# Decode attention on one core: one staging copy on POOL in place of four, and the last result copied and sent by ACT

## The chip, the cores and the metric

The kernel runs on one core of one Trainium2 chip. The metric is the device time of one execution in microseconds (us). Before the change it was 246.51 us, the median of three runs (246.47 to 246.59). Differences in this study are tenths of a microsecond, about 0.1%, so kernels are compared within rounds on the same chip, five executions each.

Engines are called PE (matmul; PEld is its weight load), DVE (vector), ACT (scalar), POOL (GpSimd) and SP (which issues 29 of this kernel's 31 DMAs). The *span* runs from the first to the last instruction of the kernel in the profile and is given to 0.1 us. The time is longer than the span (246.43 us against 244.6 us in the profiled run of the kernel before). The difference is called "outside the span" below.

## The reference

Two decode attentions, A and B, stand side by side, each with one query token of width 576, 32 query heads, 16 key/value heads of width 128 and a cache of 8192 keys. A looks at the last 2048 keys only, B at all of them.

```python
# x: [1,1,576]; k_cache, v_cache: [1,16,8192,128]; wq: [576,4096]; wo: [4096,576]
q = (x @ wq).reshape(1, 1, 32, 128).transpose(0, 2, 1, 3)
k = jnp.repeat(k_cache[:, :, Sk - W:, :], 2, axis=1)      # A: W = 2048; B: all 8192
v = jnp.repeat(v_cache[:, :, Sk - W:, :], 2, axis=1)
p = softmax(jnp.einsum("bhqd,bhkd->bhqk", q, k) * 128 ** -0.5)
o = jnp.einsum("bhqk,bhkd->bhqd", p, v)
out = o.transpose(0, 2, 1, 3).reshape(1, 1, 4096) @ wo     # A and B are joined
```

## The kernel before

The work runs in five groups: group 0 is all of A, groups 1 to 4 are four key/value heads of B each. The keys of a group lie in two slots. PE turns key blocks, ACT and DVE copy the turned blocks out of PSUM, PE multiplies them with the queries (the scores), softmax follows, and PE multiplies with the values. At the end the output weights are applied, for A (`P = 0`) and then for B (`P = 1`).

Before the scores of a slot can run, POOL puts the queries of that slot into a sparse matrix `qst`, in four small copies:

```python
def q_stage(g, s):
    def go(pool):
        for e in range(2):
            for x in range(2):
                o = s * 514 + e * 260 + x * 128
                if g:      # a group of B
                    dst = bass.AP(tensor=qst, offset=o, ap=[[1024, 128], [40, 4], [1, 2]])
                    src = bass.AP(tensor=qcol, offset=HQ + 8 * (g - 1) + 4 * e + 2 * s,
                                  ap=[[2 * HQ, 128], [0, 4], [1, 2]])
                else:      # A
                    ...    # cut: the same with another pattern
                ins = pool.tensor_copy(dst, src)
        return ins
    add("pool", go, reads=[("qcol", min(g, 1))], writes=[("qst", s)], tag="q%d" % s)
```

`add` records the instruction with what it reads and writes, and the semaphores follow from that. The results leave like this:

```python
def finish_out(P):
    n = OUTS[P]
    add("dve", lambda dve: dve.tensor_copy(outsb[0:32 * n, P, 0:DM // n], ktps[P][0:32 * n, 0:DM // n]),
        reads=[("bank", P)], writes=[("outsb", P)])
    def put(eng):
        ...                # cut: source and destination of 1152 bytes
        return eng.dma_start(dst, src)
    add("sp", put, reads=[("outsb", P)], writes=[("out", P)], dma="out%d" % P)

# cut: after all is recorded
prog.emit()                # every engine's program; at its end a barrier of all engines
for P in range(2):
    o = prog.writer[("out", P)]
    nc.sync.wait_ge(prog.sem(o.key), o.value)       # SP waits for both outputs to land
```

Of the kernel before, what the change touches and what calls it, by code (L numbers as in the profile page):

```python
# [7 lines left out]
ACT = mybir.ActivationFunctionType  # L8
AX = mybir.AxisListType

HQ = 32
HKV = 16
DH = 128
DM = 576
# [22 lines left out]
class Program:  # L37
# [15 lines left out]
    def add(self, eng, fn, reads=(), writes=(), dma=None, after=(), tag=None, inc=1, loop=None):  # L53
        op = Op(eng, fn, tuple(reads), tuple(writes), dma, tag, inc if dma is None or inc > 1 else 16, loop)
        deps = []
        for r in op.reads:
            w = self.writer.get(r)
            if w is not None:
                deps.append((w, True))
            if r[0] == "bank":  # L60
                deps += [(o, False) for o in self.readers.get(r, ())]
        for r in after:
            deps += [(o, False) for o in self.readers.get(r, ())]
        for r in op.writes:
            w = self.writer.get(r)
            if w is not None:
                deps.append((w, False))
            deps += [(o, False) for o in self.readers.get(r, ())]
        for r in op.reads:
            self.readers.setdefault(r, []).append(op)  # L70
        for r in op.writes:
            self.writer[r] = op
            self.readers[r] = []
        for o, raw in deps:
            if o is op:
                continue
            if o.dma is None and o.eng == eng and (not raw or eng in ("pe", "sp")):
                continue
            op.deps.append(o)
            o.needed = True  # L80
        op.order = len(self.ops)
        self.ops.append(op)
        return op
# [192 lines left out]
def bass_concat_heads__sliding_block_cached__gqa_block_cached__decode_kernel(  # L276
# [30 lines left out]
    prog = Program(nc)  # L307
    add = prog.add
# [14 lines left out]
    qst = nc.alloc_sbuf_tensor("qst", [128, 1024], BF16)  # L323
    qcol = nc.alloc_sbuf_tensor("qcol", [128, 2, HQ], BF16)
# [15 lines left out]
    outsb = nc.alloc_sbuf_tensor("outsb", [128, 2, DM // 2], BF16)  # L340
    warm = nc.alloc_sbuf_tensor("warm", [128, 8], F32)

    ktps = [nc.alloc_psum_tensor("ktps%d" % b, [128, 512], F32) for b in range(4)]
# [73 lines left out]
    def load_v(g):  # L417
# [19 lines left out]
        reads=["ident"], writes=["twice"])  # L437
    add("pe", lambda pe: pe.matmul(misc[:, 320:338], lhsT=twice[:, :], rhs=xnine[:, :, :].rearrange("p a r -> p (a r)"),  # L438
                                   start=True, stop=True),
        reads=[("xnine", 0), ("xnine", 1), "twice"], writes=[B_M])  # L440
# [34 lines left out]

    def q_stage(g, s):
        def go(pool):
            for e in range(2):
                for x in range(2):
                    o = s * 514 + e * 260 + x * 128  # L480
                    if g:
                        dst = bass.AP(tensor=qst, offset=o, ap=[[1024, 128], [40, 4], [1, 2]])
                        src = bass.AP(tensor=qcol, offset=HQ + 8 * (g - 1) + 4 * e + 2 * s, ap=[[2 * HQ, 128], [0, 4], [1, 2]])
                    else:
                        dst = bass.AP(tensor=qst, offset=o, ap=[[1024, 128], [80, 2], [40, 2], [1, 2]])
                        src = bass.AP(tensor=qcol, offset=8 * x + 4 * e + 2 * s, ap=[[2 * HQ, 128], [16, 2], [0, 2], [1, 2]])
                    ins = pool.tensor_copy(dst, src)  # L487
            return ins
        add("pool", go, reads=[("qcol", min(g, 1))], writes=[("qst", s)], tag="q%d" % s)
# [206 lines left out]

    def finish_out(P):
        n = OUTS[P]
        add("dve", lambda dve: dve.tensor_copy(outsb[0:32 * n, P, 0:DM // n], ktps[P][0:32 * n, 0:DM // n]),  # L699
            reads=[("bank", P)], writes=[("outsb", P)])  # L700

        def put(eng):
            src = bass.AP(tensor=outsb, offset=P * DM // 2, ap=[[32 * DM, n], [1, DM // n]])
            dst = out[0, 0:1, P * DM:(P + 1) * DM].rearrange("o (j n) -> (o j) n", j=n)
            return eng.dma_start(dst, src)
        add("sp", put, reads=[("outsb", P)], writes=[("out", P)], dma="out%d" % P)


    WQ = [(4 * SLOT - WQ_W, [("v", 2)]), (SLOT, [("k", 1, 0), ("k", 1, 1), ("v", 0)])]
    for P in range(2):  # L710
# [11 lines left out]
        reads=["kindA"], writes=["sameA"])  # L722
# [3 lines left out]
        reads=["sameB0"], writes=["sameB"])  # L726
# [3 lines left out]
    def pick_A(dve):  # L730
# [8 lines left out]
        reads=["sameB0", "pickB"], writes=["pickB"])  # L739
# [3 lines left out]
        reads=["four"], writes=["maskP"])  # L743
# [35 lines left out]
    for P in range(2):  # L779
        for Q, lo, n, off, res in wo_loads:  # L780
            if Q == P:
                wo_part(P, lo, n, off, res)
        finish_out(P)
    prog.emit()
    for P in range(2):
        o = prog.writer[("out", P)]
        nc.sync.wait_ge(prog.sem(o.key), o.value)

# [1 line left out]
_INS = ['A_x', 'A_k_cache', 'A_v_cache', 'A_wq', 'A_wo', 'B_x', 'B_k_cache', 'B_v_cache', 'B_wq', 'B_wo']  # L790
# [24 lines left out]
```

## Time and profile before

| | before |
|---|---|
| time, median of 3 runs | 246.51 us |
| span of the profiled run | 244.6 us (its time: 246.43 us) |
| read from memory | 102.76 MB, 420 GB/s over the span |
| PE, DVE, ACT, POOL busy | 67%, 36%, 38%, 4% |
| staging copies on POOL | 40, of 191 ns |

First, lines of the page: the busy time of each engine, then, in 40 equal slices of the span, the busy share of the DMA engines in tenths, then the queue that carries the loads with its packets, megabytes and share of time.

```profile
PE 163.9 (67%) x2325; PEld 119.5 (49%) x2325; DVE 88.2 (36%) x152; ACT 92.5 (38%) x95; POOL 9.1 (4%) x57
DMA  8999999999999999899999999998989999989993
q1 hardware_dynamic: 3900, 102.76, 98.1%
q14 instruction: 2, 0.02, 0.0%
```

The digits of 8 and 9 say that the loads hardly pause (their queue holds 98.1% of the DMA engines' time), and no engine comes near 100% (PE has 67%): the kernel is bound by its loads. Only in the last slice do they run out (a digit of 3). The line of queue 14 counts two fetches of instructions.

Next, the table of windows: for each stretch the busy time of each engine with its number of instructions, the granted PE clock, the DMA share and the rate in GB/s.

```profile
core 0: us, PE busy (x) PEld busy (x) DVE busy (x) ACT busy (x) POOL busy (x), PEclk, DMA share, GB/s
178.00:217.00 39.00, 29.87 (x397) 21.61 (x394) 15.01 (x22) 17.59 (x18) 0.00 (x0) 0.80 1.00 432
233.00:242.50 9.50, 6.95 (x204) 5.49 (x200) 2.35 (x4) 0.00 (x0) 0.00 (x0) 1.00 0.78 322
242.50:244.60 2.10, 0.02 (x4) 0.00 (x0) 0.31 (x1) 0.00 (x0) 0.00 (x0) 1.00 0.00 1
```
After 242.5 us no load moves any more, only the last result is left. Then POOL's timeline, four copies merged into a line (start, length, instruction, and in brackets the idle time before and who ended it), and the list of waits for the same copies (total us, times, longest):

```profile
48.92 0.56 POOL L487 COPY qst<-qcol 128x8 bf16<-128x8 bf16 x4 [23.68 <-PE sacc L522]
62.63 0.56 POOL L487 COPY qst<-qcol 128x8 bf16<-128x8 bf16 x4 [13.15 <-PE sacc L522]
```

```profile
POOL qst L487 <- PE sacc L522: 145.2, 8, 30.9
```

POOL waits for PE's scores, since the queries of the group before are in use until then. Nobody is listed as waiting for POOL. Last, the end of the timeline: PE's last products, the copy out of PSUM, and the issue of the last DMA.

```profile
241.33 1.19 PE L691 MATMUL ktps<-slots,opj 128*32 128x144 bf16 x46 [0.72 <-issue]
242.57 0.31 DVE L699 CAST outsb<-ktps 128x144 bf16<-128x144 f32 x1 [2.78 <-PE ktps L691]
242.91 0.57 SPq L705 DMA_DIRECT2D out_dram<-outsb  x1
```

### The profile page before, as it was taken

How to read it: one execution, taken by the hardware profiler on the slowest of the kernel's cores; microseconds unless marked ns; L12 is line 12 of the kernel's file. 1: busy time of each engine (PE TensorE's matmuls, PEld its weight loads, DVE VectorE, ACT ScalarE, POOL GpSimd, SP SyncE). 2: the span in 40 equal slices, each digit the busy share in tenths (PEclk: the TensorE clock that was granted, in tenths of full speed). 3: DMA queues.
4: the chain of work that ended last, by engine and by line, in shares of the span. 5: the costliest groups of instructions: out<-in, count | busy, mean ns of one | idle time of the engine just before them, and what ended most of it. 6: DMA issues, size and time to landing. Idle time of an engine off the chain costs nothing. (4 is left out here: it accounts for less than half of the span.)

```text
span 244.6 us, 5235 instructions
## 1 busy us (share of the span) xinstructions
PE 163.9 (67%) x2325; PEld 119.5 (49%) x2325; DVE 88.2 (36%) x152; ACT 92.5 (38%) x95; POOL 9.1 (4%) x57
## 2 busy tenths in 40 slices
PE   0007339968389995393999162999457799945965
PEld 0002139746236773233866121987232787624854
DVE  0001306854316454204655302455322245543031
ACT  2000016855306786102876300687600378630000
POOL 5000100000000000000000000000000000000000
PEclk9999957997759999569999859799957589975599
DMA  8999999999999999899999999998989999989993
GB/s 313 458 404 419 431 434 426 429 426 431 450 426 430 482 397 461 375 434 429 489 429 429 423 418 429 439 498 386 472 380 429 429 488 397 461 388 422 416 411 137
DMA packets 4068, 102.88 MB, mean 421 GB/s; under 512 B 602, under 2 KB 732, under 8 KB 988
## 3 DMA queue, kind: packets, MB, share of 16 engines
q1 hardware_dynamic: 3900, 102.76, 98.1%
q8 instruction: 6, 0.10, 0.2%
q10 hardware_dynamic: 160, 0.00, 0.0%
q14 instruction: 2, 0.02, 0.0%
HBM read 102.76 MB, written 0.00 MB: 420 GB/s over the span
## 5 line engine op out<-in xcount | busy, mean ns | idle before, releaser
L507 ACT ACTIVATE kt<-ktps 128x1024 bf16<-128x1024 bf16 x80 | 79.3, 1037 | 90.0 <-PE ktps L497 89.9
L497 PE MATMUL ktps<-ident,slots 128*128 128x128 bf16 x1280 | 86.5, 232 | 22.6 <-PEq L214 19.1
L497 PEld LDWEIGHTS ktps<-ident,slots 128*128 128x128 bf16 x1280 | 80.3, 105 | 38.2 <-issue 38.2
L510 DVE COPY kt<-ktps 128x1024 bf16<-128x1024 bf16 x80 | 60.8, 768 | 57.7 <-PE ktps L497 57.6
L589 PE MATMUL opsum<-slots,ptm 128*32 128x512 bf16 x320 | 29.0, 539 | 11.4 <-PEq L214 11.4
L522 PE MATMUL sacc<-kt,qst 128*32 128x512 bf16 x320 | 25.4, 392 | 2.1 <-PEq L214 2.1
L589 PEld LDWEIGHTS opsum<-slots,ptm 128*32 128x32 bf16 x320 | 14.0, 129 | 24.8 <-issue 22.8
L560 PE MATMUL misc<-ident,psb 128*128 128x128 bf16 x40 | 4.4, 276 | 15.8 <-PEq L214 15.8
L607 DVE TENSOR_TENSOR vtmp<-opsum,maskV 128x512 f32<-128x512 f32 x4 | 2.8, 692 | 32.0 <-PE opsum L589 32.0
L548 ACT ACTIVATE psb<-sacc,stat 128x2048 bf16<-128x2048 f32 x5 | 9.8, 1967 | 10.2 <-DVE stat L537 10.2
L560 PEld LDWEIGHTS misc<-ident,psb 128*128 128x128 bf16 x40 | 3.3, 122 | 18.2 <-issue 18.2
L438 PE MATMUL misc<-xnine,twice 64*128 64x18 bf16 x1 | 0.2, 172 | 17.8 <-DMA xnine<-in_B_x_dram 17.8
L487 POOL COPY qst<-qcol 128x8 bf16<-128x8 bf16 x40 | 5.5, 191 | 165.0 <-PE sacc L522 145.2
L567 DVE TENSOR_TENSOR ptm<-misc,maskP 128x1024 bf16<-128x1024 bf16 x5 | 3.5, 692 | 15.8 <-PE misc L560 15.8
L522 PEld LDWEIGHTS sacc<-kt,qst 128*32 128x32 bf16 x320 | 5.0, 94 | 8.3 <-issue 4.8
L438 PEld LDWEIGHTS misc<-xnine,twice 64*128 64x128 bf16 x1 | 0.1, 103 | 17.8 <-issue 17.8
L462 ACT ACTIVATE qrow<-opsum 128x512 bf16<-128x512 f32 x1 | 0.6, 597 | 19.2 <-PE opsum L456 19.2
L691 PE MATMUL ktps<-slots,opj 128*32 128x144 bf16 (+1 forms) x192 | 6.6, 247 | 0.7 <-issue 0.7
L691 PEld LDWEIGHTS ktps<-slots,opj 128*32 128x32 bf16 x192 | 5.3, 96 | 1.8 <-issue 0.9
L447 DVE TENSOR_SCALAR xpad<-misc,par 128x5 bf16<-128x5 f32 (+1 forms) x8 | 1.2, 230 | 13.6 <-PE misc L438 13.6
L535 DVE TENSOR_REDUCE stat<-sacc 128x1 f32<-128x512 f32 x5 | 3.5, 692 | 4.4 <-PE sacc L522 4.4
L560 PE MATMUL turned<-ident,psb 128*128 128x128 bf16 x40 | 4.8, 294 | 0.0
(74 smaller groups left out, 51.5 us busy)
## 6 DMA issues: line engine op xcount, KB each, us to landing
slots<-in_B_k_cache_dram SPq DMA_DIRECT2D x8, 4096.0 KB
slots<-in_A_k_cache_dram SPq DMA_DIRECT2D x4, 2048.0 KB
slots<-in_A_v_cache_dram SPq DMA_DIRECT2D x4, 2048.0 KB
slots<-in_A_wq_dram SPq DMA_DIRECT2D x1, 4608.0 KB, 13.7
slots<-in_B_wq_dram SPq DMA_DIRECT2D x1, 4608.0 KB, 23.8
slots<-in_A_wo_dram SPq DMA_DIRECT2D x1, 4608.0 KB, 18.6
slots<-in_B_wo_dram SPq DMA_DIRECT2D x1, 3024.0 KB, 25.4
slots<-in_B_wo_dram SPq DMA_DIRECT2D x1, 1008.0 KB, 7.6
```

The lines of the kernel that those rows point to most:

```text
L487: ins = pool.tensor_copy(dst, src)
L497: ins = pe.matmul(ktps_bf[q][:, t * 128:(t + 1) * 128], lhsT=slots[:, o:o + 128], rhs=ident[:, :], start=True, stop=True, is_transpose=True)
L507: add("act", lambda act, src=src, dst=dst: act.activation(dst, src, ACT.Copy), reads=[("bank", q)], writes=[("kt", u % NKT, q)], tag="e%d% ...
L510: add("dve", lambda dve, src=src, dst=dst: dve.tensor_copy(dst, src), reads=[("bank", q)], writes=[("kt", u % NKT, q)], tag="e%d%d" % (u, q))
L522: ins = pe.matmul(sacc[32 * j:32 * j + 32, :], lhsT=qst[:, o:o + 32], rhs=rhs, start=(u == 0 and e == 0), stop=True, skip_group_check=True)
L535: add("dve", lambda dve: dve.tensor_reduce(st(C_M + g), sacc[:, :], AX.X, ALU.max), reads=[B_S], writes=[("st", C_M + g)], tag="max")
L548: return act.activation(dst, src, ACT.Exp, bias=st(C_NB + g), scale=SCALE, accum_out=st(C_L + g))
L560: ins = pe.matmul(dst[:, t * 128:(t + 1) * 128], lhsT=psb[:, o:o + 128], rhs=ident[:, :], start=True, stop=True, is_transpose=True)
L567: return dve.tensor_tensor(ptm[:, c * 1024:(c + 1) * 1024].rearrange("p (t y) -> p t y", t=8), dst.rearrange("p (t y) -> p t y", t=8), mas ...
L589: ins = pe.matmul(opsum[64 * j + 32 * x:64 * j + 32 * x + 32, :], lhsT=ptm[:, o:o + 32], rhs=v[:, at[0], at[1], :, :, b:b + 128], start=(n ...
L607: add("dve", lambda dve: dve.tensor_tensor(vtmp[:, :, :], src, by, ALU.mult), reads=[B_O, w], writes=["vtmp"], tag="keep")
L691: ins = pe.matmul(ktps[P][32 * j:32 * j + 32, 0:w], lhsT=opj[:, P, jj:jj + 32], rhs=slots[:, o:o + w], start=(jj == 0), stop=(jj == HQ - 1))
```

## The change

The intent was to give POOL less to do (one copy for the queries of a slot of B, where there were four), and to shorten the end by letting ACT copy the last result and send it from its own queue, with no other engine in between. The final wait for that output moves to ACT too.

```diff
     def q_stage(g, s):
         def go(pool):
-            for e in range(2):
-                for x in range(2):
-                    ...                                  # cut: four copies, as above
+            if g:
+                dst = bass.AP(tensor=qst, offset=s * 514, ap=[[1024, 128], [260, 2], [128, 2], [40, 4], [1, 2]])
+                src = bass.AP(tensor=qcol, offset=HQ + 8 * (g - 1) + 2 * s, ap=[[2 * HQ, 128], [4, 2], [0, 2], [0, 4], [1, 2]])
+                return pool.tensor_copy(dst, src)
+            ...                                          # cut: A's four copies, in another order
@@ finish_out
-        add("dve", lambda dve: dve.tensor_copy(outsb[0:32 * n, P, 0:DM // n], ktps[P][0:32 * n, 0:DM // n]), ...)
+        to, of = outsb[0:32 * n, P, 0:DM // n], ktps[P][0:32 * n, 0:DM // n]
+        if P:
+            add("act", lambda act: act.activation(to, of, ACT.Copy), reads=[("bank", P)], writes=[("outsb", P)])
+        else:
+            add("dve", lambda dve: dve.tensor_copy(to, of), reads=[("bank", P)], writes=[("outsb", P)])
-        add("sp", put, reads=[("outsb", P)], writes=[("out", P)], dma="out%d" % P)
+        add("act" if P else "sp", put, reads=[("outsb", P)], writes=[("out", P)], dma="out%d" % P)
@@ after emit
-        nc.sync.wait_ge(prog.sem(o.key), o.value)
+        (nc.scalar if P else nc.sync).wait_ge(prog.sem(o.key), o.value)
```

More of the change, by code (lines that the diff above doesn't have):

```diff
@@ L477, in go @@
         def go(pool):
-            for e in range(2):
-                for x in range(2):
-                    o = s * 514 + e * 260 + x * 128
-                    if g:
-                        dst = bass.AP(tensor=qst, offset=o, ap=[[1024, 128], [40, 4], [1, 2]])
-                        src = bass.AP(tensor=qcol, offset=HQ + 8 * (g - 1) + 4 * e + 2 * s, ap=[[2 * HQ, 128], [0, 4], [1, 2]])
-                    else:
-                        dst = bass.AP(tensor=qst, offset=o, ap=[[1024, 128], [80, 2], [40, 2], [1, 2]])
-                        src = bass.AP(tensor=qcol, offset=8 * x + 4 * e + 2 * s, ap=[[2 * HQ, 128], [16, 2], [0, 2], [1, 2]])
+            if g:
+                dst = bass.AP(tensor=qst, offset=s * 514, ap=[[1024, 128], [260, 2], [128, 2], [40, 4], [1, 2]])
+                src = bass.AP(tensor=qcol, offset=HQ + 8 * (g - 1) + 2 * s, ap=[[2 * HQ, 128], [4, 2], [0, 2], [0, 4], [1, 2]])
+                return pool.tensor_copy(dst, src)
+            for x in range(2):
+                for e in range(2):
+                    dst = bass.AP(tensor=qst, offset=s * 514 + e * 260 + x * 128, ap=[[1024, 128], [80, 2], [40, 2], [1, 2]])
+                    src = bass.AP(tensor=qcol, offset=8 * x + 4 * e + 2 * s, ap=[[2 * HQ, 128], [16, 2], [0, 2], [1, 2]])
                     ins = pool.tensor_copy(dst, src)
@@ L698, in finish_out @@
         n = OUTS[P]
-        add("dve", lambda dve: dve.tensor_copy(outsb[0:32 * n, P, 0:DM // n], ktps[P][0:32 * n, 0:DM // n]),
-            reads=[("bank", P)], writes=[("outsb", P)])
+        to, of = outsb[0:32 * n, P, 0:DM // n], ktps[P][0:32 * n, 0:DM // n]
[3 more added lines that the diff above has]
+            add("dve", lambda dve: dve.tensor_copy(to, of), reads=[("bank", P)], writes=[("outsb", P)])
         def put(eng):
```

## The prediction

> **What bounds the kernel.** It streams caches and weights. The page says 102.76 MB read at 420 GB/s over a span of 244.6 us; the load queue holds 98.1% of the DMA engines' time. The windows give a DMA share of 0.97 to 1.03 in every stretch from 20 to 233 us, with PE about 70% busy and POOL 0 to 4%. From 242.5 us to the end the DMA moves about 1 GB/s. A change that neither moves bytes nor releases a load earlier can only act in those last 2 us.
>
> **Staging on POOL.** Five groups times two slots times four copies are 40 copies of 128x8, 190 ns each; four take 0.56 us from first start to last end (timeline of POOL). For B's groups, 32 copies become 8 of four times the size; I estimate 0.2 to 0.25 us for one, as a 128x128 memset on POOL takes 0.20 us. Each staging ends about 0.3 us sooner, 2.6 us of POOL time in all. None is on the path: POOL waits 145.2 us for PE's scores, the answer for the copies' line names nobody who waited for them, and the chain of waits holds no POOL work. The set for slot 1 at 62.6 us is needed only when that slot's scores of the next group run, well over 10 us later. Worth: 0. A's copies stay and merely change order.
>
> **The last copy.** In the timeline, the last matmul ends near 242.5, DVE casts 128x144 from 242.57 to 242.88 (309 ns), SP issues the last DMA at 242.91 for 0.57 us, and the span ends at 244.6: 1.7 us from the start of issue. ACT's PSUM copies took 1037 ns for 1024 columns and 597 for 512: 0.86 ns each and a base of 157 ns, so I estimate 280 ns for 144. [...] Gain over DVE: 0 to 0.03 us. The trace has one table load though Copy and Exp alternate, so no new load comes; ACT has been idle since 222.3 us.
>
> **The last issue.** ACT still waits for its own copy's semaphore before it issues, so the hop of about 0.03 us remains. ACT's two issues at the start took 0.54 and 0.61 us, SP's last took 0.57: equal. [...] SP's queue is not occupied then: it issued the first output 3 us earlier, and the last weights have landed. So landing should cost the same, and the final wait moves from SP to ACT. Worth: -0.1 to +0.2 us.
>
> **Predicted.** 246.4 us, 8 times in 10 between 245.9 and 247.0, mostly the spread between chips and runs. Faster by over 2%: 0.01; within 2%: 0.97; slower by over 2%: 0.02.
>
> **What would show it.** POOL: 16 staging copies instead of 40, the merged ones near 0.2 us, POOL busy down from 9.1 to about 6 us, nobody waiting for them. DMA share and GB/s unchanged. At the end: an ACT copy of 0.28 to 0.31 us about 0.05 us after PE, an ACT issue of about 0.6 us some 0.03 to 0.1 us later, and 1.0 to 1.3 us from there to the end.
>
> **What would make it wrong.** A slower start of a queue unused for 240 us; ACT's copy finishing its write later than the record shows; a longer end of the program on ACT than on SP; a POOL copy with four free dimensions that takes over 10 us. Any but the last costs tenths of a microsecond, not 5 us.

What its terms come to: staging 0, the copy 0 to 0.03 us, the last issue -0.1 to +0.2 us, together between 0.1 us lost and 0.23 us gained on 246.51 us, against which it puts 246.4 us.

## More of the kernel before

At the barrier after the last instructions, POOL collects: it waits until the four other engines have arrived, then releases them. The wait and the release are two instructions, one after the other, in POOL's program; the trace has them at 244.04 and 244.48 us from the span's start. SP's final waits come after this barrier, at 244.59 us.

## The result, and the profile after

| | before | after |
|---|---|---|
| time, median of 6 runs each | 246.47 us (246.35 to 246.59) | 246.17 us (246.10 to 246.28) |
| ratio | 1 | 0.9989 (95%: 0.9976 to 1.0001) |
| span of the profiled run | 244.6 us | 244.4 us |

A ratio is the mean time of one kernel's runs over that of the other's of the same rounds, so not quite the ratio of the medians. By the interval the two kernels are the same. The twelve single runs do not overlap, however, and 0.3 us of difference call for a reason. The lines after, in the order of those before; first the page:

```profile
PE 163.6 (67%) x2325; PEld 119.5 (49%) x2325; DVE 87.9 (36%) x151; ACT 93.1 (38%) x96; POOL 6.3 (3%) x33
DMA  8999999999999999899999999999999999989993
q1 hardware_dynamic: 3892, 102.76, 98.1%
q14 instruction: 2, 0.02, 0.0%
```

POOL has 24 instructions fewer and 2.8 us less work; the loads are as before. The windows (the last two end 0.2 us earlier, as the span does):

```profile
core 0: us, PE busy (x) PEld busy (x) DVE busy (x) ACT busy (x) POOL busy (x), PEclk, DMA share, GB/s
178.00:217.00 39.00, 29.27 (x394) 21.17 (x393) 15.01 (x22) 17.78 (x18) 0.00 (x0) 0.80 1.00 434
233.00:242.30 9.30, 6.87 (x200) 5.54 (x200) 2.26 (x4) 0.00 (x0) 0.00 (x0) 1.00 0.78 321
242.30:244.40 2.10, 0.08 (x4) 0.00 (x0) 0.00 (x0) 0.29 (x1) 0.00 (x0) 1.00 0.00 1
```

POOL's timeline and its wait:

```profile
48.70 0.21 POOL L481 COPY qst<-qcol 128x32 bf16<-128x32 bf16 x1 [23.52 <-PE sacc L521]
60.31 0.21 POOL L481 COPY qst<-qcol 128x32 bf16<-128x32 bf16 x1 [11.40 <-PE sacc L521]
```

```profile
POOL qst L481 <- PE sacc L521: 147.4, 8, 30.5
```

The merged copy takes 0.21 us for the 0.56 us of four, and POOL still only waits. The end:

```profile
241.78 0.60 PE L690 MATMUL ktps<-slots,opj 128*32 128x144 bf16 x16 [0.43 <-DMA slots<-in_B_wo_dram]
242.43 0.29 ACT L700 ACTIVATE outsb<-ktps 128x144 bf16<-128x144 f32 x1 [20.24 <-PE ktps L690]
242.75 1.08 ACTq L707 DMA_DIRECT2D out_dram<-outsb  x1
```

ACT's copy is 0.02 us shorter than DVE's was. The record of the issue is 1.08 us long, against 0.57 us on SP. By the trace's semaphore records the last piece of the output landed at 244.40 us, 1.65 us after the start of the issue; before, it was 244.54 us, 1.63 us after. So the longer record did not delay the output; what it did delay comes to light below.

Nothing here accounts for 0.3 us clearly. Single executions of the kernel before had spans from 244.4 to 244.9 us, so a difference of 0.2 us between two profiled runs tells little.

### The profile page after: what moved, and what is told of

Read it like the earlier page. It is cut to its first block, busy times and chain, and to the rows that moved or that the text cites. A ratio compares the mean times of both kernels' runs of the same rounds, so it can differ in the third digit from the quotient of the medians. Undisturbed runs are those within 1.5% of the kernel's fastest.

```text
span 244.4 us, 5212 instructions
## 1 busy us (share of the span) xinstructions
PE 163.6 (67%) x2325; PEld 119.5 (49%) x2325; DVE 87.9 (36%) x151; ACT 93.1 (38%) x96; POOL 6.3 (3%) x33
## 5 line engine op out<-in xcount | busy, mean ns | idle before, releaser
L588 PE MATMUL opsum<-slots,ptm 128*32 128x512 bf16 x320 | 28.5, 532 | 13.6 <-PEq L214 13.6
L481 POOL COPY qst<-qcol 128x32 bf16<-128x32 bf16 x8 | 1.7, 212 | 147.4 <-PE sacc L521 147.4
L559 PE MATMUL turned<-ident,psb 128*128 128x128 bf16 x40 | 5.3, 313 | 0.0
```

The costliest lines, as they stand in the source:

```text
L481: return pool.tensor_copy(dst, src)
L559: ins = pe.matmul(dst[:, t * 128:(t + 1) * 128], lhsT=psb[:, o:o + 128], rhs=ident[:, :], start=True, stop=True, is_transpose=True)
L588: ins = pe.matmul(opsum[64 * j + 32 * x:64 * j + 32 * x + 32, :], lhsT=ptm[:, o:o + 32], rhs=v[:, at[0], at[1], :, :, b:b + 128], start=(n ...
```

## The experiments

Twelve kernels ran, in three calls of four; each call shares one chip and nine executions of the kernel before. All gave correct results. In the table, all times are means; "outside" is the mean over the same five executions of the time less the span. The number of POOL's instructions is counted in the compiled program.

| run | POOL instr. | last output by | time | before, same call | span | outside |
|---|---|---|---|---|---|---|
| before (three calls) | 70 | SP | 246.42 to 246.49 | | 244.58 to 244.63 | 1.84 to 1.86 |
| e1_staging_only | 46 | SP | 246.08 | 246.47 | 244.62 | 1.46 |
| e2_tail_only | 70 | ACT | 246.57 | 246.47 | 244.70 | 1.87 |
| e3_act_copy_sp_queue | 70 | SP | 246.43 | 246.47 | 244.56 | 1.87 |
| e4_dve_copy_act_queue | 70 | ACT | 246.67 | 246.47 | 244.86 | 1.81 |
| f1_merged_pad24 | 70 | SP | 246.53 | 246.42 | 244.62 | 1.91 |
| f2_merged_pad12 | 58 | SP | 246.02 | 246.42 | 244.54 | 1.48 |
| f3_before_pad24 | 94 | SP | 246.10 | 246.42 | 244.60 | 1.50 |
| f4_after_sp_queue | 46 | SP | 245.98 | 246.42 | 244.50 | 1.48 |
| h1_after | 46 | ACT | 246.28 | 246.49 | 244.64 | 1.64 |
| h2_act_queue_sp_wait | 46 | ACT | 246.11 | 246.49 | 244.50 | 1.61 |
| h3_slow_staging | 61 | SP | 246.49 | 246.49 | 244.64 | 1.85 |
| h4_after_sp_queue | 46 | SP | 245.94 | 246.49 | 244.44 | 1.50 |

Outside the span, the executions of one kernel lie within 0.2 us of each other, and the means of the same kernel in two or three calls agree within 0.02 us. The row of the changed kernel's own six executions, which ran elsewhere, would read 246.18 us, span 244.52 us, outside 1.66 us.

### First call: which half of the change?

The first theory (T) was that the gain comes from the end, because only the end is free of the loads. The rivals were that earlier staging helps the loads (S), and noise (N).

**e1_staging_only** is the kernel before with the new `q_stage`; the end is untouched.

> Only the merged staging copies on POOL; the end is that of before. Theory T (the 0.3 us come from the end of the program, after the last matmul): same as before within 0.1 us. Rival S (the gain comes through the loads: queries staged 0.35 us sooner shift something that releases a load): faster by 0.2 to 0.4 us. Rival N (noise of a few executions): no difference beyond 0.1 us here and in the other three runs. All: POOL busy 6.3 us, merged copies 0.21 us each.

Measured: 246.11 us median against 246.48 us, ratio 0.9983 (0.9969 to 0.9996). Theory T is refuted: the whole gain, and a little more, is here. Rival S foresaw the size, but the span did not shorten (mean 244.62 us, before 244.63 us). The 0.38 us went from *outside* the span: 1.46 us instead of 1.84 us. A shift in the loads, which in the kernel before end by 242.5 us of the 244.6, would have shown in the span.

**e2_tail_only** is the kernel before with the other half: ACT's copy, ACT's queue and the wait on ACT.

> Only the end: the last copy on ACT, its DMA and the last wait on ACT's queue; staging as before. Theory T: faster by 0.2 to 0.4 us, as the whole change. Rival S and rival N: same as before within 0.1 us. In the profile, the ACT issue takes about 1.1 us as in the changed kernel and 1.6 to 1.7 us pass from the start of issue to the end of the span.

Measured: 246.52 us against 246.48 us, ratio 1.0004 (0.9990 to 1.0017). The end that the change was meant to shorten is worth nothing in this kernel.

**e3_act_copy_sp_queue** has ACT copy and SP send and wait:

```diff
-        add("act" if P else "sp", put, ...)          # against e2
+        add("sp", put, ...)
-        (nc.scalar if P else nc.sync).wait_ge(...)
+        nc.sync.wait_ge(...)
```

> The end with the copy on ACT, but sent from SP and awaited by SP. Theory T in the form that ACT's copy is what helps: faster by 0.02 to 0.1 us (ACT copy 0.29 us for DVE's 0.31). T in the form that the queue or the place of the last wait helps: same within 0.05 us. S and N: same.

Measured: 246.46 us against 246.48 us, ratio 0.9994 (0.9981 to 1.0008). The 0.02 us by which ACT's copy is shorter cannot be told from nothing.

**e4_dve_copy_act_queue** has DVE copy and ACT send and wait (`if P:` becomes `if False:` in e2).

> The end with DVE's copy, but sent from ACT's queue and awaited by ACT. Theory T in the form that queue or last wait helps: faster by 0.2 to 0.3 us. T in the form of the copy: same within 0.05 us. S and N: same. If the issue takes 1.1 us on ACT here too, the length belongs to ACT's queue and not to the copy before it.

Measured: 246.70 us against 246.48 us, ratio 1.0007 (0.9994 to 1.0021). ACT's queue brings no gain. The line of the issue in this run's timeline:

```profile
242.95 1.08 ACTq L708 DMA_DIRECT2D out_dram<-outsb  x1
```

It is 1.08 us long here too, so the length belongs to the issue on ACT and not to the copy ahead of it.

### What the timeline does not show: the barrier

The timeline lists no semaphore instructions, but the trace holds them, with the semaphore updates and the fetches of instructions by DMA. Read from these, the end of each profiled run falls into pieces that repeat to 0.01 us. In the table, *arrival* is when the engine that sent the last output reaches the barrier (it is the last to do so), *release* is when POOL lets the engines go (POOL takes the last arrival 0.05 us after it in all runs), *step* is the third update of the semaphore that the end sequence uses once the kernel's own program is over (245.11 us from the span's start in the kernel before; its updates follow each other in the same order in every run), and *last* is the last semaphore update of the execution. "fetch" is the time of any 8192-byte instruction fetch on queue 14, from the span's start, other than two that every kernel has at 77 to 80 us and at 120 to 124 us.

```
                    POOL   last   issue to  arrival to  release  step to   issue
run                 instr. DMA by  arrival   release    to step   last    to last  fetch
before                70   SP       1.10      0.49       0.61     1.43     3.64    245.16
e2_tail_only          70   ACT      1.28      0.49       0.61     1.52     3.91    245.16
e3_act_copy_sp_queue  70   SP       1.10      0.49       0.61     1.43     3.63    245.34
e4_dve_copy_act_queue 70   ACT      1.29      0.49       0.61     1.43     3.82    245.38
after                 46   ACT      1.28      0.13       0.56     1.43     3.41    none
e1_staging_only       46   SP       1.10      0.13       0.56     1.43     3.22    none
-- second and third call --
f1_merged_pad24       70   SP       1.10      0.48       0.61     1.43     3.63    245.46
f2_merged_pad12       58   SP       1.10      0.13       0.56     1.43     3.22    none
f3_before_pad24       94   SP       1.10      0.13       0.56     1.43     3.23    27.61
f4_after_sp_queue     46   SP       1.10      0.13       0.56     1.43     3.23    none
h1_after              46   ACT      1.28      0.13       0.56     1.43     3.41    none
h2_act_queue_sp_wait  46   ACT      1.28      0.13       0.56     1.43     3.41    none
h3_slow_staging       61   SP       1.10      0.13       0.56     1.53     3.32    none
h4_after_sp_queue     46   SP       1.10      0.13       0.56     1.43     3.23    none
```

After the first call the first six rows were known. They hold two differences and no more. First, with 70 instructions POOL takes 0.49 us from the last arrival to the release, and 0.05 us more afterwards; with 46 it takes 0.13 us. The 0.36 us lie between two neighbouring instructions of POOL, the wait and the release: from start to start 0.44 us in the kernel before and 0.08 us in the changed one. Second, an engine that sends the last output arrives 1.10 us after the start of the issue if it is SP and 1.28 us after it if it is ACT. On SP that is the issue (0.57 us) and a drain of 0.47 us with small gaps; on ACT the issue (1.08 us) and a drain of 0.15 us. Both differences are there whatever the other is: 3.64 us from the issue to the end with SP and 70 instructions, 3.22 us with SP and 46, 3.82 us with ACT and 70 (e4), 3.41 us with ACT and 46.

The landing of the output is not in this sum. With ACT as sender it lies 0.33 us ahead of the step in the changed kernel, with SP 0.17 us ahead (e1), and both take the step 0.56 us after the release. So the release of the barrier is enough to set the step in all of them; with ACT the landing clearly does not. With SP it does not either: in the six kernels with SP and a short release the step comes 0.564 us after the release each time, while its distance to the landing varies from 0.165 to 0.179 us. The step is followed by 1.43 us to the last update, or by 0.09 to 0.10 us more in e2 and h3, for no reason that the records show.

The first difference led to theory F: it is not the *work* of the staging copies that counts but the *place* of POOL's last instructions in its program, which the number of instructions before them shifts. In the trace the late release goes with one more fetch of instructions, of 8192 bytes, on queue 14 (at 245.16 us in the kernel before; others, of 16384 bytes, are on queue 8). No record names the engine that a fetch serves. That POOL waits for one was the guess, which no run shows.

### Second call: work or place?

**f1_merged_pad24** is e1 with 24 instructions given back to POOL that do nothing of use and run when POOL has nothing else to do. (**f2** has 12 of them; **f3** adds 24 to the kernel before.)

```diff
+    pad = nc.alloc_sbuf_tensor("pad", [128, 64], F32)
+    def padding(pool):
+        for i in range(24):
+            ins = pool.memset(pad[:, i:i + 1], 0.0)
+        return ins
+    add("pool", padding, writes=["pad"])              # after the set-up at 4 us
```

> Merged staging, and 24 tiny memsets of an unread tile on POOL at about 4 us, where POOL idles, so that POOL's program has again as many instructions as before. Theory F [...]: slow again, as before within 0.1 us; 0.44 us from the last arrival to the release, 1.84 us outside the span, and an 8192-byte instruction fetch after 245 us. Rival S (queries staged sooner help): fast as with merged staging alone, 0.3 to 0.45 us faster than before, release after 0.08 us.

Measured: 246.45 us against 246.40 us, ratio 1.0002 (0.9988 to 1.0015). The gain is gone, although the queries are staged in one copy, as early as in e1. The line of the memsets in this run's timeline shows that they are over at 5.2 us, long before the first staging copy at 24.4 us:

```profile
4.30 0.86 POOL L393 MEMSET pad<- 128x1 f32 x24
24.44 1.06 POOL L493 COPY qst<-qcol 128x8 bf16<-128x8 bf16 x8 [19.28 <-DVE xpad L454]
```

From arrival to release it takes 0.48 us again, the fetch after the span is back, and 1.91 us lie outside. Rival S is refuted.

> Merged staging with 12 such memsets. Theory F, a step: either all of the 0.37 us or none (release after 0.08 or 0.44 us). Rival G, a cost per POOL instruction: half, 0.19 us faster than before. Rival S: fast.

Measured: 245.93 us against 246.40 us, ratio 0.9982 (0.9969 to 0.9996), release 0.13 us after arrival. Half the instructions cost nothing at all: a step, and no cost per instruction.

> The kernel before with 24 such memsets, so POOL's program is longer by 24 instructions. Theory F: once the place lies before the barrier, [...] fast, 0.3 to 0.45 us faster than before and release after 0.08 us, if 24 are enough to move it there; else as before. Rival G: slower than before by 0.37 us. Rival S: same as before within 0.1 us.

Measured: 245.97 us against 246.40 us, ratio 0.9989 (0.9975 to 1.0002), release 0.13 us after arrival, 1.50 us outside. This is the strangest and the most telling run: *more* POOL instructions than before, with all forty copies in place, and the 0.34 us outside the span are gone. A fetch now stands inside the span, at 27.61 us, and not after 175 us, where the guess had put it. At 27.61 us POOL had 58 of its 93 recorded instructions behind it, while in the kernel before the fetch came after all 69 (the traces record one fewer than the compiled program has). The page of this run shows it as a third packet:

```profile
q14 instruction: 3, 0.02, 0.0%
```

**f4_after_sp_queue** is the changed kernel with the last output sent and awaited by SP:

```diff
-        add("act" if P else "sp", put, ...)
+        add("sp", put, ...)
-        (nc.scalar if P else nc.sync).wait_ge(...)
+        nc.sync.wait_ge(...)
```

> The changed kernel, but the last output is sent and awaited by SP. If ending on ACT costs what the traces suggest (0.33 us from landing to the end barrier on ACT, 0.17 on SP), 0.1 to 0.2 us faster than the changed kernel, that is 0.4 to 0.5 us faster than before, with 1.46 us outside the span. If ACT's queue is free of cost: 0.3 us faster than before, as the changed kernel.

Measured: 245.94 us against 246.40 us, ratio 0.9984 (0.9970 to 0.9997), 1.48 us outside. The changed kernel had 1.66 us outside in the executions of the result. It is level with f2 (medians 245.94 and 245.93 us), so ACT's copy adds nothing that can be told from scatter. The next call sets it beside the changed kernel.

### Third call: ACT's end, and is staging really off the path?

**h1_after** is the changed kernel once more.

> The changed kernel again, beside the next two on one chip. 0.25 to 0.35 us faster than before; 0.33 us from the last semaphore update of the last output to the next step of the end sequence, 1.6 to 1.7 us outside the span.

Measured: 246.28 us against 246.47 us, ratio 0.9992 (0.9978 to 1.0006), 1.64 us outside.

**h2_act_queue_sp_wait** changes only who waits for ACT's output:

```diff
-        (nc.scalar if P else nc.sync).wait_ge(...)
+        nc.sync.wait_ge(...)
```

> The changed kernel, its last output still sent from ACT, but awaited by SP. Theory W (it is the wait on ACT that makes the end longer[...]): 0.15 us faster than the changed kernel, 0.17 us after landing, 1.45 to 1.5 us outside the span. Theory Q (it is ACT's queue): as the changed kernel.

Measured: 246.07 us against 246.47 us, ratio 0.9985 (0.9971 to 0.9998). Its mean is 0.17 us below h1's, but 0.14 us of that are in the span (244.50 and 244.64 us), which scatters by as much between executions. Outside it has 1.61 us, as h1 (1.64 us), not 1.45 to 1.5 us, and from the issue to the last update it takes 3.41 us, as h1 to the hundredth. By the times alone theory W would have looked right; by the end of the trace it is refuted: it does not matter which engine waits. Sending from ACT is what costs, because ACT is then the last to reach the barrier, 1.28 us after the start of its issue. Why the same issue takes ACT 1.08 us and SP 0.57 us stays open.

**h3_slow_staging** is e1 with each staging copy held back by a memset that waits for the same scores:

```diff
+        if g:
+            add("pool", lambda pool: pool.memset(pad[:], 0.0),          # pad: 128 x 4096 bf16
+                reads=["pad"], writes=["pad", ("qst", s)], tag="pad")
         add("pool", go, ..., writes=[("qst", s)], tag="q%d" % s)
```

> Merged staging of B, each copy held back by a memset of an unread 128x4096 bf16 tile on POOL that waits for the same scores, about 4 us by the 0.95 us that 128x1024 took: queries are staged ten times later than the change staged them sooner. POOL's program has 8 instructions more than with merged staging alone, fewer than the 12 that cost nothing. Staging off the path (the prediction, and theory F): same as merged staging alone, 0.3 to 0.45 us faster than before. Rival S: slower than before by some us.

Measured: 246.44 us against 246.47 us, ratio 0.9999 (0.9985 to 1.0013), which is not what staging off the path was said to give. The timeline shows that the delay worked:

```profile
61.45 3.51 POOL L490 MEMSET pad<- 128x4096 bf16 x1 [9.69 <-PE sacc L524]
64.91 0.21 POOL L482 COPY qst<-qcol 128x32 bf16<-128x32 bf16 x1
88.50 3.51 POOL L490 MEMSET pad<- 128x4096 bf16 x1 [23.38 <-PE sacc L524]
91.95 0.21 POOL L482 COPY qst<-qcol 128x32 bf16<-128x32 bf16 x1
```

Staging 3.5 us later left the span as it was: 244.64 us, and 244.62 us in e1 and in the kernel before of the same call. So staging is off the path, as predicted. Yet the time rose by 0.4 us over e1, again outside the span (1.85 us). POOL releases the barrier 0.13 us after the last arrival here, so this is not the same stall. In the profiled run the time is 0.28 us longer than the stretch from the span's start to the last recorded semaphore update (246.62 less 246.34); in the other kernels it is between 0.12 us shorter and 0.02 us longer. POOL's program has 61 instructions, not the 54 counted on, because seven of the added waits became instructions of their own. Whether a place between those of f2 (58, no stall) and f1 (70, a stall at the release) moves the stall to the very end, no run has tested.

**h4_after_sp_queue** is f4 again, beside h1.

> The changed kernel with the last output sent and awaited by SP, beside the changed kernel on the same chip: 0.15 us faster than it and 0.4 to 0.5 us faster than before. If the difference is only a chip's or a run's: equal to it within 0.05 us.

Measured: 245.99 us (245.77 to 246.09) against 246.47 us for the kernel before (246.29 to 246.75) and 246.28 us for the changed one (246.18 to 246.36) on the same chip. The ratio to before is 0.9978 (0.9964 to 0.9991). It beats both kernels, by 0.55 us and 0.34 us in the means (246.49 and 246.28 less 245.94). Of the 0.34 us to the changed kernel, the pieces at the barrier explain 0.18 us (3.41 less 3.23); the rest is in the part of the span ahead of the last issue, and the other kernels do not bear it out (the means of the span are 244.52 and 244.50 us in after and h2, with ACT's queue, and 244.50 us in f4 without). The end of h4's timeline:

```profile
242.44 0.29 ACT L700 ACTIVATE outsb<-ktps 128x144 bf16<-128x144 f32 x1 [20.24 <-PE ktps L690]
242.75 0.57 SPq L707 DMA_DIRECT2D out_dram<-outsb  x1
```

## Why the prediction was right or wrong

**The time and its class were right.** 246.17 us lie within 245.9 to 247.0, near the 246.4 foretold, and the kernels count as the same. That says little for the reasoning: the range is 1.1 us wide, the largest effect found here is 0.42 us, and the two terms that were mis-sized have opposite signs. What bounds the kernel was right too: the loads, untouched by the change.

**Staging: the durations were right, the worth was wrong.** Sixteen copies, 0.21 us each for the merged ones, POOL busy 6.3 us, nobody waiting: as predicted. That the *time* of the copies is off the path was shown by h3, whose span did not move when staging came 3.5 us later. But the step "None is on the path ... Worth: 0" failed for the change as a whole. Removing 24 instructions was worth 0.42 us at the end (3.64 us less 3.22 us from issue to last update; 246.47 less 246.08 is 0.39 us in the times), by their number and not by their work. f1 gave the instructions back without the work and lost the gain; f3 added still more and had it again. The prediction asked what the copies cost as work and never what they do as places in a program, and it looked for effects within the span alone.

**The last copy was right.** ACT took 0.29 us (0.28 estimated from its two measured sizes, 0.28 to 0.31 foretold) and began 0.02 us after PE.

**The last issue was wrong, in its length and in its worth.** "ACT's two issues at the start took 0.54 and 0.61 us, SP's last took 0.57: equal" failed: the issue on ACT took 1.08 us in the after trace and in e2, e4, h1 and h2. The output landed no later for it, 1.65 us after the start of the issue against 1.63 us, but the landing, 0.33 us ahead of the step, is not what the end waits for last. ACT reached the barrier 0.18 us later than SP would have (1.28 less 1.10 us). The prediction counts a gain as positive worth, so "-0.1 to +0.2 us" allowed a loss of 0.1 us at most; the loss of 0.18 us lies outside, and the term that was mis-sized is this issue. Nor did "1.0 to 1.3 us" pass from the issue to the end of the span: it was 1.69 us from the issue's start and 0.60 us from its end. "A longer end of the program on ACT than on SP" was on the list of what could go wrong, and it went wrong in this way: by the sending, not by the wait that moved.

**The two parts add.** From the last issue to the end the change saves 0.42 us by POOL's place and loses 0.19 us by ACT's issue, which makes 0.23 us (3.64 less 3.41). The times agree: 0.21 us in the means of h1 (246.49 less 246.28), 0.30 us between the medians of the first comparison. e2 and e4, with ACT's loss alone, are 0.10 and 0.20 us slower than before in the means; f4 and h4, with POOL's gain alone and ACT's copy, 0.44 and 0.55 us faster. How a loss divides between the span and the rest says little by itself: in e2 and e4 it lengthens the span, whose last instruction is the wait after the barrier, and in the changed kernel it lies outside.

**What stays open.** That the number of POOL's instructions, apart from their work, decides the stall is shown by f1, f2 and f3. That the stall is a wait for instructions is not shown. The fetch on queue 14 is there after the span in all five kernels that stall at the release and in none of the others. But it *starts* 0.66 us after the release in the kernel before (245.16 us less 244.50 us), so it cannot be the very wait that ended then. Nor, if both serve POOL, does one fixed place in its program, counted from the start, describe this fetch and the one of f3, which came after fewer instructions. So theory F holds for the number of instructions, and its reason stays open. What POOL does in the 0.44 us between its two instructions no record shows. h3's loss is open too: 0.10 us of it lie between the step and the last update, and in the profiled run another 0.26 to 0.40 us after the last update (0.28 us longer, where the other kernels are 0.12 us shorter to 0.02 us longer).

## What to carry to other kernels

When a change of a few tenths of a microsecond surprises you, split each run's time into the span and the rest, and look at the barrier at the end, before you seek the reason among the instructions that the timeline lists: here every gain and loss that could be told from scatter lay there, but for that of h3, which came later still. Adding or removing instructions on POOL, 3 to 4% busy, shifted the release here by a step of 0.36 us that had nothing to do with their work, so repeat the comparison with useless instructions added before you credit the optimization. And undo each half of a change alone: here one half gained by accident, and the other, which was meant to shorten the end, lengthened it.
